# One row of an output-projection weight loaded by four smaller DMAs, and a shorter last sum, in a one-token decode kernel

## The chip, the core and the metric

The kernel runs on one core of one Trainium2 chip. A core has a matrix engine (PE in the profile, with its weight loads as PEld), a vector engine (DVE), a scalar engine (ACT), a general engine (POOL) and a sync engine (SP). SP and ACT issue the loads here; the bytes of all loads are moved by the core's 16 DMA engines. The metric is the device time of one execution in microseconds (us).

## What is computed

One token of width 1024 passes through two branches, which are added to the input. `xn` is the layer-normalised input.

```python
xn = _layernorm(x)
# attention over the last 4096 cached positions: 32 query heads, 4 key/value heads, head size 128
q = (xn @ wq)                                  # wq: 1024 x 4096
p = _softmax(q . k_cache[last 4096] * 128**-0.5)
o = p . v_cache[last 4096]                     # 32 heads x 128 = 4096 numbers
A = o @ wo                                     # wo: 4096 x 1024
# channel MLP
h = _gelu(_layernorm(xn) @ w1 + b1)            # w1: 1024 x 3584
B = h @ w2 + b2                                # w2: 3584 x 1024
out = x + A + B
```

The kernel computes in bfloat16 with float32 sums. With one token there is nothing to reuse: every weight and every cached key and value is read once, 39.9 MB in all.

## The kernel before, in words

**Loads.** All large loads are issued by SP in program order: the keys (four loads), wq (two), w1 (two), the values (three), w2 (two), wo (six). Each puts its matrix on 128 partitions. They go into a ring of four buffers of 32 KB per partition (`ring_tile`, line 64), so that a load waits until the work on the buffer's earlier content is done. The framework gives each DMA one of eight completion semaphores in rotation; a DMA waits until the DMA that used its semaphore before has landed. ACT issues three loads of single rows at the start: x, b2 and b1 (lines 75 to 78).

**wo.** wo has 4096 rows of 1024. Row `32 p + c` lies on partition `p` as its row `c` (`wo_v`, line 222), so each partition holds 32 rows of 2 KB, and a product with one column `c` of a 128 x 32 matrix `o8` takes one such row of all partitions at once. The first half (rows 0 to 15, buffer `wo0`) comes by one DMA, the second half (`wo1`) by five, of 8, 4, 2, 1 and 1 rows (lines 223 to 229), so that the last products wait for little.

**Attention.** The keys are transposed by DVE and copied by DVE and ACT (lines 184 to 201). Query, scores, softmax and the product with the values `o_all` (line 319) follow. DVE scales and gathers the result into `o_bf`, 32 heads x 128 (lines 322 to 326). Element `128 h + d` of the concatenated heads belongs to partition `p = 4 h + d // 32` and column `c = d % 32` of `o8`; four small products with a 0/1 matrix `spread` make `o8` of `o_bf` (lines 327 to 331). `spread` is made by POOL early on (lines 108 to 111), among POOL's other constants and before its two short steps `rstd` of the layer norms (lines 145 and 168).

**The last sum.** The 28 rows of w2 and the 32 rows of wo form a list `chunk_src` of 60 entries. All but the last `TAIL = 8` are summed into `accf`: two halves of 512 columns, each half in its own 32-row group of the matrix engine (lines 336 to 339), one row of output in partition 0 and one in partition 32. Then four copies, by DVE and ACT in turn, bring `accf` to `bulk`, in four pieces of 256 columns on partitions 0, 32, 64 and 96 (lines 344 to 350). The last eight rows, those that the second to fifth DMA of `wo1` bring, are summed into `acct` in four groups of 256 columns (lines 351 to 354). One addition of `acct` and `bulk` on DVE gives `res` (line 356), which SP stores as four rows of 512 bytes (line 357).

The matrix engine takes its instructions in the order of the program: w2's rows, then wo's rows 0 to 31. A group of products that waits for a load holds up all that follow.

Of the kernel before, what the change touches and what calls it, by code (L numbers as in the profile page):

```python
# [8 lines left out]
FP32 = mybir.dt.float32  # L9
BF16 = mybir.dt.bfloat16  # L10
ACT = mybir.ActivationFunctionType
ALU = mybir.AluOpType
# [4 lines left out]
def kernel(  # L17
# [14 lines left out]
    nc = tc.nc  # L32
    P = 128
    D = A_x.shape[-1]
# [4 lines left out]
    Hq = NQ // Dh  # L39
# [8 lines left out]
    CWO = NQ // P  # L48
    TAIL = 8
    NH = Fd // 8  # L50
# [4 lines left out]
    consts = ctx.enter_context(tc.tile_pool(name="consts", bufs=1))  # L55
# [4 lines left out]
    ps_f = ctx.enter_context(tc.tile_pool(name="ps_f", bufs=2, space=bass.MemoryType.PSUM))  # L60
# [23 lines left out]
    for i in range(2):  # L84
        t = ring_tile(f"wq{i}")
        tv = t[:].rearrange("p (r n) -> p r n", r=4)
# [23 lines left out]
    nc.gpsimd.affine_select(out=spread[:], in_=spread[:], compare_op=ALU.not_equal, fill=1.0, base=0,  # L110
                            pattern=[[-1, 4], [1, P]], channel_multiplier=-4)

    gmask = consts.tile([Hq, Hkv], FP32)
# [108 lines left out]
    wo_v = A_wo.rearrange("(p c) n -> p c n", p=P)  # L222
    for i, cuts in enumerate([[0, 16], [0, 8, 12, 14, 15, 16]]):
        nr = CWO // 2
        t = ring_tile(f"wo{i}")
        tv = t[:].rearrange("p (r n) -> p r n", r=nr)
        for a, b in zip(cuts[:-1], cuts[1:]):
            nc.sync.dma_start(out=tv[:, a:b, :], in_=wo_v[:, nr * i + a:nr * i + b, :])  # L228
        chunk_src += [("o", nr * i + r, tv[:, r, :]) for r in range(nr)]


    for i, w3 in enumerate(wq_tiles):
        for r in range(4):
            c = 4 * i + r
# [91 lines left out]
    nc.vector.tensor_copy(out=o_bf[:], in_=o_f[:])  # L326
    o8_ps = ps_f.tile([P, 32], FP32, tag="pf", name="o8_ps")
    for q in range(4):
        nc.tensor.matmul(o8_ps[:], lhsT=spread[:, q, :], rhs=o_bf[:, 32 * q:32 * q + 32], start=(q == 0), stop=(q == 3))
    o8 = consts.tile([P, 32], BF16)  # L330
    nc.vector.tensor_copy(out=o8[:], in_=o8_ps[:])

# [3 lines left out]
    for idx, (kind, c, wap) in enumerate(chunk_src[:n_bulk]):  # L336
        for half in range(2):
            nc.tensor.matmul(accf[32 * half:32 * half + 1, :], lhsT=vec[kind](c), rhs=wap[:, half * 512:(half + 1) * 512],  # L338
                             start=False, stop=(idx == n_bulk - 1), tile_position=(0, 32 * half))
    acct = ps_f.tile([P, 256], FP32, tag="pf", name="acct")  # L340
# [47 lines left out]
```

## Time and profile before

| | |
|---|---|
| median of three runs | 102.23 us (102.08 to 102.32) |
| the profiled execution's own time | 102.15 us |
| its span, from the first to the last instruction | 100.4 us |
| mean granted clock of the matrix engine | 0.846 |
| bytes moved, mean rate over the span | 39.92 MB, 397 GB/s |
| matrix engine busy | 45.7 us (45%) |
| DVE busy | 49.2 us (49%) |
| ACT busy | 34.2 us (34%) |
| POOL busy | 4.0 us (4%) |
| first of wo's second-half DMAs issued | 70.34 us |
| last addition (line 356) | 97.43 to 97.86 us |

All times of a profile are us from the first instruction; "L338" is line 338 of the kernel. A row of the timeline gives start, duration, engine, line, operation, output and inputs, shape and count, and in brackets how long the engine had been idle and what ended that. A row of the windows gives a stretch and its length, the busy time of PE, PEld, DVE, ACT and POOL with the number of instructions, the granted clock of the matrix engine, the mean busy share of the 16 DMA engines, and GB/s. Beside these views the trace holds every packet of a DMA (start, duration, size, queue) and every step of a completion semaphore. It does not say on which of the 16 DMA engines a packet ran.

### The profile page before, as it was taken

To read this page: it belongs to the slowest core of one execution; us is meant where nothing else is said; L and a number is where in the kernel's file an instruction comes from. 1 tells how busy PE (TensorE), PEld (TensorE's weight loads), DVE (VectorE), ACT (ScalarE), POOL (GpSimd) and SP (SyncE) were. 2 spreads that over 40 slices of the span, in tenths; PEclk is the share of its full clock that TensorE was granted. 3 is DMA by queue.
4 is the path that set the end of the run, shared out by engine and by line. 5 is a ranking of instruction groups with operands and counts; after the bars stand their busy time and mean duration, and the time that the engine had idled before them with its cause. 6 is when DMAs were issued, how large, how long until landed. Compare 5 with 4: busy or idle time off the path is not lost.

```text
span 100.4 us, 976 instructions
## 1 busy us (share of the span) xinstructions
PE 45.7 (45%) x369; PEld 18.0 (18%) x369; DVE 49.2 (49%) x91; ACT 34.2 (34%) x37; POOL 4.0 (4%) x17
## 2 busy tenths in 40 slices
PE   0472000009500920297462009999199910299640
PEld 0422000003100300024221003334133400033210
DVE  4616799999999999992552460000900000000310
ACT  2300008999999999902204630000000000000100
POOL 6024200000000000000000000000000000000000
PEclk9999999999999997559999655589957995559975
DMA  2999999999999998999999998989989999999900
GB/s 40 375 431 434 499 431 496 431 418 418 418 418 392 468 440 369 502 400 400 390 440 424 424 506 388 509 377 423 480 388 414 418 444 437 437 405 401 382 33 1
DMA packets 2882, 39.92 MB, mean 397 GB/s; under 512 B 311, under 2 KB 315, under 8 KB 702
## 3 DMA queue, kind: packets, MB, share of 16 engines
q1 hardware_dynamic: 2872, 39.85, 93.3%
q8 instruction: 3, 0.05, 0.2%
q10 hardware_dynamic: 6, 0.01, 0.0%
q14 instruction: 1, 0.01, 0.0%
HBM read 39.86 MB, written 0.00 MB: 397 GB/s over the span
## 4 chain that ended last, share of the span: by engine, by line
DVE 39%; DMA 25%; PE 15%; issue 8%; ACT 5%; POOL 3%; SPq 2%; POOLq 1%; ACTq 0%; DVEq 0%
DMA wo<-in_A_wo_dram 25%; DVE kt_scr L185 17%; DVE kT L201 16%; PE o_all L319 10%; PE sp L275 2%; DVE hT L314 2%; SPq L228 2%; PE acch L257 2%; ACT L312 1%; ACT e L297 1%; DVE eTb L299 1%; DVE m_loc L283 1%; ACT h_sb L312 1%; DVE q_sb L240 1%; POOLq L383 1%
## 5 line engine op out<-in xcount | busy, mean ns | idle before, releaser
L199 ACT COPY kT<-kt_scr 32x1024 bf16<-32x1024 bf16 x26 | 27.1, 1042 | 12.2 <-DVE kt_scr L185 12.0
L185 DVE STREAM_TRANSPOSE kt_scr<-k_sb 128x4096 bf16<-128x4096 bf16 x4 | 17.4, 4409 | 0.0
L201 DVE COPY kT<-kt_scr 32x1024 bf16<-32x1024 bf16 x38 | 15.9, 419 | 0.5
L237 PE MATMUL accq<-wq,xnT 128*1 128x512 bf16 x64 | 6.9, 607 | 19.5 <-DMA wq<-in_A_wq_dram 19.5
L350 ACT COPY bulk<-accf 1x256 f32<-1x256 f32 x2 | 0.7, 361 | 36.3 <-DVE bulk L348 36.3
L319 PE MATMUL o_all<-v_sb,eTb 128*32 128x512 bf16 x32 | 9.9, 484 | 5.4 <-DVE hT L314 5.4
L348 DVE COPY bulk<-accf 1x256 f32<-1x256 f32 x2 | 0.8, 416 | 21.6 <-PE accf L338 21.1
L338 PE MATMUL accf<-wo,o 128*1 128x512 bf16 x48 | 6.8, 449 | 6.5 <-DMA wo<-in_A_wo_dram 6.5
L338 PE MATMUL accf<-w,hT 128*1 128x512 bf16 x56 | 8.1, 452 | 0.1
L257 PE MATMUL acch<-w,yT 128*1 128x448 bf16 x64 | 4.8, 463 | 6.3 <-DMA w<-in_B_w_dram 6.3
L237 PEld LDWEIGHTS <-xnT 128*1 128x1 bf16 x64 | 2.1, 116 | 23.8 <-issue 23.8
L319 PEld LDWEIGHTS <-eTb 128*32 128x32 bf16 x32 | 3.7, 117 | 11.2 <-DVE hT L314 5.5
L322 DVE TENSOR_TENSOR o_m<-o_all,grs 32x512 f32<-32x512 f32 x1 | 0.7, 679 | 10.0 <-PE o_all L319 10.0
L338 PEld LDWEIGHTS <-o 128*1 128x1 bf16 x48 | 2.4, 94 | 10.9 <-issue 8.8
L338 PEld LDWEIGHTS <-hT 128*1 128x1 bf16 x56 | 2.8, 96 | 4.9 <-issue 2.7
L257 PEld LDWEIGHTS <-yT 128*1 128x1 bf16 x64 | 1.7, 99 | 9.0 <-issue 8.3
L314 DVE STREAM_TRANSPOSE hT<-h_sb 128x896 bf16<-128x896 bf16 x1 | 1.7, 1699 | 2.4 <-ACT h_sb L312 2.4
L297 ACT ACTIVATE e<-sc,nmx 128x1024 bf16<-128x1024 f32 x1 | 1.1, 1147 | 3.9 <-DVE nmx L294 3.9
L353 PE MATMUL acct<-wo,o 128*1 128x256 bf16 x32 | 1.7, 283 | 1.7 <-DMA wo<-in_A_wo_dram 1.7
L275 PE MATMUL sp<-kT,qm 128*32 128x512 bf16 x32 | 2.1, 380 | 0.3 <-DVE qm L266 0.3
L104 ACT ACT_TABLE_LOAD x1 | 1.3, 1283 | 1.9 <-issue 1.9
L299 DVE STREAM_TRANSPOSE eTb<-e 128x1024 bf16<-128x1024 bf16 x1 | 1.2, 1246 | 1.4 <-ACT e L297 1.4
(85 smaller groups left out, 32.2 us busy)
## 6 DMA issues: line engine op xcount, KB each, us to landing
w<-in_B_w_dram SPq DMA_DIRECT2D x4, 3584.0 KB, 23.7
wq<-in_A_wq_dram SPq DMA_DIRECT2D x2, 4096.0 KB, 19.9
k_sb<-in_A_k_cache_dram SPq DMA_DIRECT2D x4, 1024.0 KB, 7.0
wo<-in_A_wo_dram SPq DMA_DIRECT2D x1, 4096.0 KB
v_sb<-in_A_v_cache_dram SPq DMA_DIRECT2D x1, 2048.0 KB
v_sb<-in_A_v_cache_dram SPq DMA_DIRECT2D x2, 1024.0 KB, 22.5
wo<-in_A_wo_dram SPq DMA_DIRECT2D x1, 2048.0 KB, 21.6
wo<-in_A_wo_dram SPq DMA_DIRECT2D x1, 1024.0 KB
```

The lines of the kernel that those rows point to most:

```text
L185: nc.vector.transpose(out=scr[:, g, :], in_=k2[:, g, :])
L199: nc.scalar.copy(out=dst, in_=src)
L201: nc.vector.tensor_copy(out=dst, in_=src)
L228: nc.sync.dma_start(out=tv[:, a:b, :], in_=wo_v[:, nr * i + a:nr * i + b, :])
L237: nc.tensor.matmul(accq[32 * t:32 * t + 1, b, :], lhsT=xnT[:, c:c + 1], rhs=w3[:, r, j * 512:(j + 1) * 512], start=(c == 0), stop=(c == C ...
L257: nc.tensor.matmul(acch[32 * t:32 * t + 1, b, :NH], lhsT=yT[:, c:c + 1], rhs=w3[:, r, j * NH:(j + 1) * NH], start=False, stop=(c == C - 1) ...
L275: nc.tensor.matmul(sp[32 * R:32 * R + 32, :], lhsT=qm[:, g, :], rhs=kT[:, g, c0:c0 + 512], start=(g == 0), stop=(g == Hkv - 1), tile_posit ...
L297: nc.scalar.activation(out=e128[:], in_=sc[:], func=ACT.Exp, bias=nmx[:], scale=scale, accum_out=l_loc[:])
L299: nc.vector.transpose(out=eTb[:], in_=e128[:])
L314: nc.vector.transpose(out=hT[:], in_=h_sb[:].rearrange("p (d c) -> p c d", c=CW2))
L319: nc.tensor.matmul(o_all[:].rearrange("h g d -> h (g d)"), lhsT=eTb[:, 32 * c:32 * c + 32], rhs=v4[:, :, c, :], start=(c == 0), stop=(c == ...
L338: nc.tensor.matmul(accf[32 * half:32 * half + 1, :], lhsT=vec[kind](c), rhs=wap[:, half * 512:(half + 1) * 512], start=False, stop=(idx == ...
```

## The change

Row 15 of `wo0` is no longer part of the large DMA, which now brings rows 0 to 14. Four DMAs of their own follow it. Two bring row 15 of partitions 0 to 95 to where it was, the first on partitions 0, 2, 4 and so on, the second on 1, 3, 5. Two bring row 15 of the other 32 partitions (96 to 127) to partitions 0 to 31 of a new buffer `wo_x`, again every second partition each. Their source is cut so that its outermost count is 12 (for the 96) or 4 (for the 32): source rows are taken in groups of four partitions, every second group by one DMA. Partition `8 e + 2 v + s` therefore holds the row of partition `8 e + 4 s + v`. A second 0/1 matrix `spread_x` with four more small products makes a 33rd column of `o8` in that order, and a copy moves its partitions 96 to 127 to partitions 0 to 31 as a 34th. The two products of row 15 become four: two over 96 partitions and two over 32. `TAIL` goes from 8 to 4: rows 24 to 27, which the 4-row DMA brings, are summed into `accf`, and four rows are left for `acct`.

```diff
--- before.py
+++ after.py
@@ -46,7 +46,7 @@
     WQ4 = W // 4
     CW2 = Fd // P
     CWO = NQ // P
-    TAIL = 8
+    TAIL = 4
     NH = Fd // 8
     eps = 1e-5
     scale = float(Dh) ** -0.5
@@ -109,6 +109,12 @@
     nc.gpsimd.memset(spread[:], 0.0)
     nc.gpsimd.affine_select(out=spread[:], in_=spread[:], compare_op=ALU.not_equal, fill=1.0, base=0,
                             pattern=[[-1, 4], [1, P]], channel_multiplier=-4)
+    spread_x = consts.tile([Hq, 4, P], BF16)
+    nc.gpsimd.memset(spread_x[:], 0.0)
+    for s in range(2):
+        sx = spread_x[:].rearrange("h q (e a s) -> h q e a s", a=4, s=2)[:, :, :, :, s]
+        nc.gpsimd.affine_select(out=sx, in_=sx, compare_op=ALU.not_equal, fill=1.0, base=4 * s,
+                                pattern=[[-1, 4], [8, 16], [1, 4]], channel_multiplier=-4)
 
     gmask = consts.tile([Hq, Hkv], FP32)
     nc.gpsimd.memset(gmask[:], 1.0)
@@ -220,12 +226,20 @@
         nc.sync.dma_start(out=tv, in_=w2_v[:, nr * i:nr * (i + 1), :])
         chunk_src += [("h", nr * i + r, tv[:, r, :]) for r in range(nr)]
     wo_v = A_wo.rearrange("(p c) n -> p c n", p=P)
-    for i, cuts in enumerate([[0, 16], [0, 8, 12, 14, 15, 16]]):
+    MOVED = 15
+    wo_x = consts.tile([32, D], BF16)
+    for i, cuts in enumerate([[0, MOVED], [0, 8, 12, 14, 15, 16]]):
         nr = CWO // 2
         t = ring_tile(f"wo{i}")
         tv = t[:].rearrange("p (r n) -> p r n", r=nr)
         for a, b in zip(cuts[:-1], cuts[1:]):
             nc.sync.dma_start(out=tv[:, a:b, :], in_=wo_v[:, nr * i + a:nr * i + b, :])
+        if i == 0:
+            wo_m = tv[:, MOVED, :]
+            for (dst, p0, ne) in ((wo_m, 0, 12), (wo_x, 96, 4)):
+                rows = A_wo[p0 * CWO:(p0 + 8 * ne) * CWO, :].rearrange("(e s v c) n -> e s v c n", e=ne, s=2, c=CWO)
+                for s in range(2):
+                    nc.sync.dma_start(out=dst[s:8 * ne:2, :], in_=rows[:, s, :, MOVED, :])
         chunk_src += [("o", nr * i + r, tv[:, r, :]) for r in range(nr)]
 
 
@@ -324,19 +338,27 @@
     nc.vector.tensor_reduce(out=o_f[:], in_=o_m[:].rearrange("h g d -> h d g"), axis=AX.X, op=ALU.add)
     o_bf = consts.tile([Hq, Dh], BF16)
     nc.vector.tensor_copy(out=o_bf[:], in_=o_f[:])
-    o8_ps = ps_f.tile([P, 32], FP32, tag="pf", name="o8_ps")
+    o8_ps = ps_f.tile([P, 33], FP32, tag="pf", name="o8_ps")
     for q in range(4):
-        nc.tensor.matmul(o8_ps[:], lhsT=spread[:, q, :], rhs=o_bf[:, 32 * q:32 * q + 32], start=(q == 0), stop=(q == 3))
-    o8 = consts.tile([P, 32], BF16)
-    nc.vector.tensor_copy(out=o8[:], in_=o8_ps[:])
+        nc.tensor.matmul(o8_ps[:, 0:32], lhsT=spread[:, q, :], rhs=o_bf[:, 32 * q:32 * q + 32], start=(q == 0), stop=(q == 3))
+    for q in range(4):
+        nc.tensor.matmul(o8_ps[:, 32:33], lhsT=spread_x[:, q, :], rhs=o_bf[:, 32 * q + MOVED:32 * q + MOVED + 1],
+                         start=(q == 0), stop=(q == 3))
+    o8 = consts.tile([P, 34], BF16)
+    nc.vector.tensor_copy(out=o8[:, 0:33], in_=o8_ps[:])
+    nc.vector.tensor_copy(out=o8[0:32, 33:34], in_=o8_ps[96:128, 32:33])
 
 
     vec = {"h": lambda c: hT[:, c, 0:1], "o": lambda c: o8[:, c:c + 1]}
     n_bulk = len(chunk_src) - TAIL
     for idx, (kind, c, wap) in enumerate(chunk_src[:n_bulk]):
-        for half in range(2):
-            nc.tensor.matmul(accf[32 * half:32 * half + 1, :], lhsT=vec[kind](c), rhs=wap[:, half * 512:(half + 1) * 512],
-                             start=False, stop=(idx == n_bulk - 1), tile_position=(0, 32 * half))
+        parts = [(vec[kind](c), wap)]
+        if kind == "o" and c == MOVED:
+            parts = [(o8[0:96, 32:33], wo_m[0:96, :]), (o8[0:32, 33:34], wo_x)]
+        for (lh, rh) in parts:
+            for half in range(2):
+                nc.tensor.matmul(accf[32 * half:32 * half + 1, :], lhsT=lh, rhs=rh[:, half * 512:(half + 1) * 512],
+                                 start=False, stop=(idx == n_bulk - 1), tile_position=(0, 32 * half))
     acct = ps_f.tile([P, 256], FP32, tag="pf", name="acct")
     nc.vector.memset(acct[:], 0.0)
     bulk = consts.tile([97, 256], FP32)
```

In the built program POOL's memset and two selects for `spread_x` stand before its first `rstd`. The semaphore rotation moves on by four. The DMAs of `wo1` then wait, in order, for the third load of the values (as well as for the buffer), for w2's first half, for w2's second half, for the first half of wo, and for the first of the four new DMAs.

## The prediction

> **What bounds the kernel now.** I read the page first. The line of transfers is at nine tenths or more almost from start to end, and the matrix engine works 45% of the span: the kernel moves 39.9 MB and ends soon after the last byte of wo is in. So I went to the last 25 us: the timeline of the matrix engine there, the windows over the same stretch, and the waits.
>
> ```profile
> 87.15 6.76 PE L338 MATMUL accf<-wo,o 128*1 128x512 bf16 x48 [6.47 <-DMA wo<-in_A_wo_dram]
> 94.45 0.61 PE L353 MATMUL acct<-wo,o 128*1 128x256 bf16 x16 [0.54 <-DMA wo<-in_A_wo_dram]
> 95.68 0.39 PE L353 MATMUL acct<-wo,o 128*1 128x256 bf16 x8 [0.62 <-DMA wo<-in_A_wo_dram]
> 96.29 0.28 PE L353 MATMUL acct<-wo,o 128*1 128x256 bf16 x4 [0.22 <-DMA wo<-in_A_wo_dram]
> 96.93 0.38 PE L353 MATMUL acct<-wo,o 128*1 128x256 bf16 x4 [0.36 <-DMA wo<-in_A_wo_dram]
> ```
>
> Each group of the last sum starts when its wo rows land; the last at 96.93. What follows (products to 97.31, the addition 97.43 to 97.86, the store, the end at 100.4) has nothing beside it. A later or earlier last landing moves the end by the same amount.
>
> ```profile
> 92.00:94.00 2.00, 1.91 (x18) 0.62 (x15) 0.05 (x1) 0.00 (x0) 0.00 (x0) 1.00 0.97 400
> 94.00:95.50 1.50, 0.61 (x16) 0.37 (x17) 0.79 (x2) 0.56 (x2) 0.00 (x0) 1.00 0.89 344
> 95.50:97.00 1.50, 0.74 (x16) 0.34 (x15) 0.00 (x0) 0.16 (x1) 0.00 (x0) 0.96 0.14 51
> ```
>
> The last two columns are the busy share of the 16 DMA engines and GB/s. Until 95.5 they are all at work; then 0.14, two or three of 16, hold the end for over a microsecond. A load over 128 partitions raises its semaphore in 16 steps, one per engine. For the last wo row the trace's records put 12 steps at 95.38 to 95.69, then 95.81, **96.25, 96.72 and 96.89**. Following the packets of one engine back (each starts where the one before ended), the three late ones lost their time to instruction packets: 16 KB at 37.07 and at 63.95, on two engines, each losing 1.42 us in all (0.92 of its own and 0.5 on the next packet), and 8 KB at 38.18 on a third (0.84). A fourth engine takes 16 KB at 95.51, when its data are in. The 95.81 engine is the one that also carried the single-row loads of x and the biases; I call it engine 0.
>
> **The change, part by part.** *The moved row.* A row of wo is 2 KB on each of 128 partitions, eight packets per engine, 0.080 us apart at the end of the trace: 0.64 us. How many engines do the four new DMAs use? The store of four rows is four 512-byte packets, x's single row one packet: the outer count sets it. The new DMAs' sources have outer counts 12, 12, 4 and 4 (their destinations 48 and 16). So I take 12 engines, eight packets over two DMAs, and then four of these with eight more. The other end is all 16 engines with eight each: then nothing moves.
>
> Terms per engine. Before, wo's first half came in 32 KB packets every 1.209 us; 28 KB packets come every 1.059, so 30 KB is 1.134 by the middle: 8 x 0.075 = 0.60 less for every engine. Added for the twelve: 8 x 0.080 and two semaphore packets of 0.006 = 0.65. Added again for the four: 0.65. **Relieved (four engines): -0.60. Middle (eight): +0.05. Loaded (four): +0.70.** Engine 0 is among the loaded, as the single rows ride on it: 95.81 + 0.70 = 96.51.
>
> [...]
>
> *Whether the late engines are the relieved ones decides all*, and no view numbers them. For it: fetches fall on four different engines, never on engine 0, as if four were set apart, and four away from engine 0 are relieved. Against: the first packets of k_sb start at 1.86 to 2.10 us on 12 engines and at 2.86 to 2.90 on four; the late engines are among the 12, and if start order were engine order the relieved would be the other four. I choose "relieved", with little over even odds against everything else: this is the weakest step.
>
> With it the last landings become 96.89 - 0.60 = 96.29, 96.12, and engine 0 at 96.51. Last: 96.51, **0.38 earlier**. The two ends of this term: -0.60 (engine 0 not loaded) and +0.70.
>
> *Four rows instead of eight in the last sum.* Rows 24 to 27 go into accf: 8 products of 512 columns replace 16 of 256. They run in pairs 0.2135 us apart at full clock, the last taking 0.38: 3 x 0.2135 + 0.38 = 1.02. Their rows landed at 94.41 on the last engine; after: engine 0, 93.24 + 0.70 = 93.94. So accf ends at 93.94 + 0.05 + 1.02 = 95.01. The four copies to bulk (DVE and ACT in turn) took 93.95 to 95.66 = 1.71; they end at 96.76. The last products end at 96.51 + 0.04 + 0.38 = 96.93. So the copies stay covered by 0.17; their cover was 1.65. If they are the later, each 0.1 us costs 0.1. PE itself: 29 pairs of wo instead of 24, from 86.55; at half clock (0.427 a pair) until 90.05, then 0.2135: it would end near 94.6, before its rows let it.
>
> *What is covered.* Pool gains a memset (0.51) and two selects of half of L110's size (0.3 to 0.63 each) ahead of the first rstd: at most 1.8 into 4.63 us of waiting.
>
> ```profile
> 7.01 0.56 POOL L145 TENSOR_TENSOR rstd<-ve,mhalf 128x1 f32<-128x1 f32 x1 [4.63 <-DVE ve L143]
> 72.37 0.25 PE L329 MATMUL o_ps<-o_bf,spread 32*128 32x32 bf16 x4 [2.06 <-DVE o_bf L326]
> ```
>
> Four more products like L329's (0.25) and one more copy of o8 (0.19) lie ahead of PE's wait of 6.47 for wo and of 21.1 us of idle DVE. SP issues four more DMAs at 0.43 each after 52.92, and idles until 70.34; its queue is deep, since wo's first packets move only at 75.5. The rotation of eight DMA semaphores shifts, so wo's second-half parts now wait: the third for w2 (landed 77.45), the fourth for the first half of wo (86.5 to 87.1), the fifth for the first moved DMA (about 87). Behind them in SP's queue stands only the store. Their first packets are wanted at 92.5, 93.8 and 94.4: over five us of cover; were it gone, a late issue would cost what it is late by.
>
> Unknown: what 2 KB packets cost that land on every second partition beside other engines' packets. From nothing to as much again on the loaded four: 0 to +0.64; no row suggests a gain. I take 0, as the 2 KB rows at the end ran 0.080 apart with 16 engines writing.
>
> **Sum:** -0.38. The profiled execution was 102.15 us (span 100.4, 1.75 around it), the median of the runs shown 102.23. 102.15 - 0.38 = 101.77, so **101.8**; its own range 101.5 to 101.95 (ends -0.60 and -0.2, when a third of the unknown cost falls on engine 0).
>
> **Rivals.** (1) *The time was in none of the relieved engines*, or only one of the two latest is relieved, or all 16 share the moved row: last landing 96.89 + 0.05 at most: 102.15 to 102.25, no change. The same comes out if the packets on the loaded engines cost over half more.
> (2) *A late engine is one of the loaded four.* Its 0.70 comes on top of the latest: 96.89 + 0.70 = 97.59, or 96.72 + 0.70 = 97.42; with the tail unchanged +0.53 to +0.70: 102.7 to 102.85. It decides as soon as an engine later than 96.19 (96.89 - 0.70) is loaded; the early start of the late engines speaks for it.
> (3) *The copies to bulk become the end*: by the sum 0.17 short; if rows 24 to 27 land after 94.1, it takes a part of the gain, and in (1) it adds nothing (97.28 against 97.36).
>
> **How the numbers follow.** Chances: forecast 0.50; (1) 0.18; (2) 0.32. (3) is inside the forecast. A measurement of this kernel can tell about 0.2% (0.2 us) from no change: faster 0.48 (the forecast less its slow end), same 0.20, slower 0.32. The range 101.5 to 102.85 takes in all three; the likeliest alone is 101.5 to 101.95.
>
> **What would show it.** Right: the last L353 group starts near 96.55 and the share of the DMA engines after 95.5 shows more engines for a shorter time; the 16 steps of the last wo row have one near 96.5 and none past it; the first moved DMA shows 12 steps. Wrong: three steps still past 96.2, in the same distance (1), or one past 97.4 (2); an addition that waits for ACT's copy and not for PE (3); or a matrix engine that waits for a wo part issued late.

## The result, and the profile after

The changed kernel takes 103.29 us (median of 4 runs, 103.09 to 103.43); the kernel before, beside it, 102.28 us (4 runs, 102.08 to 102.34). The ratio is 1.0105 with a 95% interval of 1.0084 to 1.0127: about 1.0 us slower, where 0.4 us faster was forecast, and outside the range given. The profiled execution took 103.09 us with a span of 101.4 us (before: 102.15 and 100.4).

The timeline of the matrix engine over the last 12 us, in the changed kernel:

```profile
87.33 5.99 PE L360 MATMUL accf<-wo,o 128*1 128x512 bf16 x32 [4.89 <-DMA wo<-in_A_wo_dram]
93.25 0.38 PE L360 MATMUL accf<-wo_x,o 32*1 32x512 bf16 x2
93.56 2.87 PE L360 MATMUL accf<-wo,o 128*1 128x512 bf16 x24
96.62 0.39 PE L375 MATMUL acct<-wo,o 128*1 128x256 bf16 x8 [0.20 <-DMA wo<-in_A_wo_dram]
97.23 0.28 PE L375 MATMUL acct<-wo,o 128*1 128x256 bf16 x4 [0.22 <-DMA wo<-in_A_wo_dram]
97.85 0.28 PE L375 MATMUL acct<-wo,o 128*1 128x256 bf16 x4 [0.34 <-DMA wo<-in_A_wo_dram]
```

The picture is that of before: each group of the last sum starts when its rows land, and the last starts at 97.85 instead of 96.93. In the records of semaphore steps the last row of wo is complete at 97.81 instead of 96.89. So the 0.92 us are there before the last product starts; its products end 0.82 later than before (98.13 for 97.31), and the addition starts 0.82 later.

The windows over the same kernel; behind the stretch and its length stand PE, PEld, DVE, ACT and POOL, and at the end the granted clock, the busy share of the DMA engines, and GB/s:

```profile
85.00:86.50 1.50, 0.00 (x0) 0.00 (x0) 0.00 (x0) 0.00 (x0) 0.00 (x0) 0.61 1.25 388
86.50:88.00 1.50, 0.67 (x4) 0.21 (x5) 0.00 (x0) 0.00 (x0) 0.00 (x0) 0.50 0.84 277
...
94.00:95.50 1.50, 1.50 (x16) 0.59 (x14) 0.00 (x0) 0.00 (x0) 0.00 (x0) 1.00 1.06 421
95.50:97.00 1.50, 1.30 (x16) 0.36 (x13) 0.41 (x1) 0.03 (x1) 0.00 (x0) 1.00 0.52 201
97.00:98.50 1.50, 0.57 (x12) 0.17 (x7) 0.67 (x2) 0.69 (x2) 0.00 (x0) 1.00 0.02 7
```

The same two first stretches in the kernel before:

```profile
85.00:86.50 1.50, 0.00 (x0) 0.00 (x0) 0.00 (x0) 0.00 (x0) 0.00 (x0) 0.50 0.84 360
86.50:88.00 1.50, 0.85 (x6) 0.26 (x7) 0.00 (x0) 0.00 (x0) 0.00 (x0) 0.50 1.15 492
```

A packet counts whole in the stretch in which it starts, so a share can pass 1.00. What is to be read is GB/s divided by the share, the rate that 16 engines have while they are busy. Before it is 360 / 0.84 = 429 and 492 / 1.15 = 428. After it is 388 / 1.25 = **310** and 277 / 0.84 = **330**, and from 94.00 on 421 / 1.06 = 397, as before the change (344 / 0.89 = 387 in the row that the prediction shows). The DMA engines are not idle; for three microseconds each byte takes about a third longer. No term of the prediction stands for this. I call it the slow spell.

The packet records show it packet by packet: the moved row's 2 KB packets take 84 ns each if they start before 85.46, then up to 209 ns. The first 16 KB packet of wo's second half starts at 84.81 and takes its usual 611 ns; the next starts at 85.16 and takes 804, and from 85.4 on, on every engine that has come to them, they take 810 to 970. At 87.46 the last packet of `wo_x` has run, and those that start then fall from 760 back to 611 ns by 88.0. All that the packets between 84.7 and 88 took beyond their usual length is 12.2 us, or 12.2 / 16 = **0.76 us per engine**.

The vector engine, and ACT's second copy, at the end of the changed kernel:

```profile
96.47 0.41 DVE L370 COPY bulk<-accf 1x256 f32<-1x256 f32 x1 [23.94 <-PE accf L360]
97.36 0.42 DVE L370 COPY bulk<-accf 1x256 f32<-1x256 f32 x1 [0.48 <-ACT bulk L372]
98.25 0.42 DVE L378 TENSOR_TENSOR res<-acct,bulk 97x256 bf16<-97x256 f32 x1 [0.47 <-ACT bulk L372]
```

```profile
97.82 0.36 ACT L372 COPY bulk<-accf 1x256 f32<-1x256 f32 x1 [0.48 <-DVE bulk L370]
```

The last copy ends at 98.18, the last products at 98.13, and the view names the copy as what the addition waited for, the sign that the prediction gave for its third rival. Before, 0.12 us lay between the products' end and the addition; here 98.13 + 0.12 = 98.25 as well. So the copies have used up all their cover, but cost nothing that can be seen in this execution.

### The profile page after: what moved, and what is told of

It reads as the page before. It is cut to its first block, busy times and chain, and to the rows that moved or that the text cites. A ratio compares the mean times of both kernels' runs of the same rounds, so it can differ in the third digit from the quotient of the medians.

```text
span 101.4 us, 982 instructions
## 1 busy us (share of the span) xinstructions
PE 47.6 (47%) x367; PEld 18.8 (19%) x367; DVE 49.6 (49%) x92; ACT 34.2 (34%) x37; POOL 6.3 (6%) x20
## 4 chain that ended last, share of the span: by engine, by line
DMA 79%; PE 12%; SPq 2%; DVE 2%; issue 1%; ACT 1%; DVEq 0%
DMA wo<-in_A_wo_dram 44%; DMA wq<-in_A_wq_dram 20%; DMA w<-in_B_w_dram 15%; PE acch L271 5%; PE accq L251 4%; PE sp L289 3%; SPq L73 2%; DVE m_loc L297 1%; PE qT_ps L275 1%; ACT sc L294 1%; DVE res L378 0%; SPq L236 0%; DVE qm L280 0%; PE acct L375 0%; PE mT_ps L299 0%
## 5 line engine op out<-in xcount | busy, mean ns | idle before, releaser
L333 PE MATMUL o_all<-v_sb,eTb 128*32 128x512 bf16 x32 | 9.2, 458 | 5.2 <-DMA v_sb<-in_A_v_cache_dram 5.2
L360 PE MATMUL accf<-wo,o 128*1 128x512 bf16 (+1 forms) x56 | 8.9, 480 | 4.9 <-DMA wo<-in_A_wo_dram 4.9
L360 PEld LDWEIGHTS <-o 128*1 128x1 bf16 (+2 forms) x58 | 2.8, 99 | 11.2 <-issue 9.8
L289 PEld LDWEIGHTS <-qm 128*32 128x32 bf16 x32 | 1.7, 112 | 1.0 <-issue 0.6
```

What stands on the lines that cost most here:

```text
L289: nc.tensor.matmul(sp[32 * R:32 * R + 32, :], lhsT=qm[:, g, :], rhs=kT[:, g, c0:c0 + 512], start=(g == 0), stop=(g == Hkv - 1), tile_posit ...
L333: nc.tensor.matmul(o_all[:].rearrange("h g d -> h (g d)"), lhsT=eTb[:, 32 * c:32 * c + 32], rhs=v4[:, :, c, :], start=(c == 0), stop=(c == ...
L360: nc.tensor.matmul(accf[32 * half:32 * half + 1, :], lhsT=lh, rhs=rh[:, half * 512:(half + 1) * 512], start=False, stop=(idx == n_bulk - 1 ...
```

## The experiments

The result left these causes open: the shorter last sum (`TAIL = 4`); the moved row's own extra packets on a few engines; and something in the way the moved row is loaded that slows all engines for a while. Later runs divide the last one further: uneven counts of engines; every second partition; which rows a DMA engine reads, or which partitions it writes, beside the other engines. The table gives all runs; "rate" is GB/s by share from the windows row of 85 to 88 us in the profiled execution, "last" the last semaphore step of wo there. Ratios are to the kernel before, which had medians of 102.11 to 102.28 beside them. The diffs show the lines that load; the lines that fit the products and `spread_x` to them are left out.

| kernel | median us | ratio (95%) | rate | last |
|---|---|---|---|---|
| before | 102.28 | | 426 | 96.89 |
| after | 103.29 | 1.0105 (1.0084 to 1.0127) | 320 | 97.81 |
| e1_tail4_only | 102.37 | 1.0021 (0.9993 to 1.0048) | 428 | 97.12 |
| e2_rows_only | 103.96 | 1.0155 (1.0094 to 1.0215) | 301 | 99.01 |
| e3_home_dest | 103.66 | 1.0147 (1.0083 to 1.0210) | 322 | 97.64 |
| e4_swapped_groups | 103.43 | 1.0103 (1.0063 to 1.0142) | 297 | 98.30 |
| e5_no_four_engine | 103.57 | 1.0111 (1.0051 to 1.0171) | 304 | 98.01 |
| e6_plain_slices | 103.73 | 1.0145 (1.0128 to 1.0162) | 313 | 98.17 |
| e7_only_four_engine | 103.74 | one run | 324 | 98.55 |
| e8_plain_row15 | 102.21 | 0.9993 (0.9980 to 1.0007) | 423 | 96.72 |
| e9_two_halves | 103.33 | 1.0132 (1.0104 to 1.0159) | 308 | 98.11 |
| e10_source_mixed | 103.26 | one run | 297 | 98.15 |
| e11_last_row_uneven | 103.09 | 1.0107 (1.0092 to 1.0121) | 426 | 97.26 |
| f4_own_source_rows | 103.31 | 1.0108 (1.0061 to 1.0155) | 309 | 98.17 |
| f1_every_second | 102.28 | 1.0003 (0.9983 to 1.0023) | 421 | 97.07 |
| f2_dest_only | 103.40 | 1.0100 (1.0066 to 1.0135) | 304 | 98.25 |
| f5_extra_home | 102.44 | 1.0014 (1.0002 to 1.0026) | 419 | 97.44 |
| f7_extra_away | 103.07 | 1.0078 (1.0057 to 1.0099) | 339 | 97.63 |

"Last" belongs to one execution, in which instruction packets come at slightly other times (the 8 KB packet at 38.18 us in the kernel before, at 37.17 in the changed kernel), and that execution can lie at either end of a kernel's runs; the rates and the medians carry the verdicts.

### The two halves of the change alone

The kernel before, with the shorter last sum only:

```diff
-    TAIL = 8
+    TAIL = 4
```

> The kernel before with four rows instead of eight in the last sum, and no moved row. Theory (the loss comes from the moved row's DMAs): the four copies to bulk end at 94.46 + 1.02 + 0.05 + 1.71 = 97.24, the last products at 97.31 as before, so 102.2 to 102.4. Rival (the shorter last sum makes the copies the end, and that is the loss): 102.9 to 103.3.

102.37 us, a ratio whose interval takes in 1, and a rate of 428: no spell, and in the median at most half a per cent for the shorter last sum. But the profiled execution, at 103.08 us the slowest of the ten, is the rival's case:

```profile
97.16 0.28 PE L353 MATMUL acct<-wo,o 128*1 128x256 bf16 x4 [0.28 <-DMA wo<-in_A_wo_dram]
```

```profile
96.61 0.41 DVE L348 COPY bulk<-accf 1x256 f32<-1x256 f32 x1 [23.75 <-PE accf L338]
98.35 0.42 DVE L356 TENSOR_TENSOR res<-acct,bulk 97x256 bf16<-97x256 f32 x1 [0.43 <-ACT bulk L350]
```

The last products end at 97.44, so the addition could have started at 97.44 + 0.12 = 97.56; it waits for the copies until 98.35, which costs 0.79 us. Rows 24 to 27 had landed at 94.67; it was the matrix engine that was late. Its pairs of products of 512 columns stood 0.43 us apart until 93.4, and 0.21 us from then on; in the kernel before the change of pace came at 90.1, in the changed kernel at 92.0. From 90 to 92 us the granted clock was 0.50 here and 0.99 in the kernel before. Two more of the ten runs took 102.98 and 103.01 us, the other seven 101.97 to 102.55; whether those two had the same cause was not recorded. So the shorter last sum makes no spell, but it can cost 0.8 us in single executions.

The changed kernel with the last sum of eight rows:

```diff
-    TAIL = 4
+    TAIL = 8
```

> The changed kernel with eight rows in the last sum again, so that only the moved row is left of the change. Theory (moved row): a spell near 85.4 to 87.5 us in which the 16 KB packets of all engines take 0.83 to 0.97 us instead of 0.61, the last wo row landing near 97.8, 103.0 to 103.3. Rival (the shorter last sum): the last row still lands near 97 and the time is 102.2 to 102.4.

103.96 us: the moved row alone is enough for all the loss, as each of the four runs (103.31 to 104.47) is slower than any of the kernel before, and the spell is there (301). In this profile the packets stayed about a tenth slower after it, too: between 88 and 92 us the rate is 381 where after has 427.

### Where the moved row lands, and who is loaded

The 32 rows of `wo_x` go to partitions 96 to 127, where they were before, instead of 0 to 31; one product pair then takes row 15.

```diff
-            for (dst, p0, ne) in ((wo_m, 0, 12), (wo_x, 96, 4)):
+            for (dst, p0, ne) in ((tv[0:96, MOVED, :], 0, 12), (tv[96:128, MOVED, :], 96, 4)):
```

> As the changed kernel, but the rows of partitions 96 to 127 stay on partitions 96 to 127 (every second one, by the same two DMAs on four engines), with one product of 128 partitions for row 15. If the slow spell comes from writing on partitions 0 to 31 beside other engines' writes, it goes away: 16 KB packets 0.61 throughout, last landing 96.95 (the engine with the 8 KB instruction packet, 96.25 + 0.70), 102.2 to 102.4. If it comes from four engines reading rows that are not their own, or from any load on four engines beside full loads, the spell stays and the time is 103.0 to 103.3.

103.66 us, rate 322: the spell is untouched. Loading another partition than the row's own is not what makes it.

The two groups are exchanged: 12 engines load partitions 32 to 127, four load 0 to 31.

```diff
-            for (dst, p0, ne) in ((wo_m, 0, 12), (wo_x, 96, 4)):
+            for (dst, p0, ne) in ((tv[32:128, MOVED, :], 32, 12), (tv[0:32, MOVED, :], 0, 4)):
```

> As the changed kernel, but the two DMAs on 12 engines bring partitions 32 to 127 and the two on four engines partitions 0 to 31, all to their own partitions. If engines serve fixed groups of partitions and only rows away from their own group are slow, the four-engine part is now at home and fast (no spell after 85.4) and the 12-engine part is the one that could be slow (its 2 KB packets over 0.10 us). If any load on four engines slows all, the spell stays as it was and the time is 103.0 to 103.3; without any spell 102.2 to 102.4.

103.43 us, rate 297. The spell doesn't depend on which rows the 12 and the four take.

### Which of the four DMAs, and whether any

Only the 12-engine pair is kept; the other 32 rows come by one plain DMA (with `TAIL = 8`).

```diff
+            for s in range(2):
+                rows = A_wo[0:96 * CWO, :].rearrange("(e s v c) n -> e s v c n", e=12, s=2, c=CWO)
+                nc.sync.dma_start(out=tv[s:96:2, MOVED, :], in_=rows[:, s, :, MOVED, :])
+            nc.sync.dma_start(out=tv[96:128, MOVED, :], in_=wo_v[96:128, MOVED, :])
```

> Row 15 without the two DMAs on four engines: partitions 0 to 95 by the two DMAs on 12 engines as changed, partitions 96 to 127 by one DMA of 32 rows on all 16 engines, two packets each; eight rows in the last sum. Theory (four engines alone with 2 KB packets while the others have gone on to 16 KB packets slow all 16): no spell, 16 KB packets 0.61 throughout; relieved engines 0.60 - 0.16 = 0.44 earlier, the others 0.21 later, the last wo row near 96.5, 101.8 to 102.1. Rival (the spell comes from the 12-engine DMAs, or from 2 KB packets of any kind in front of 16 KB packets): the spell stays and the time is 103 to 104.

103.57 us, rate 304. Only the four-engine pair is kept, and the 96 rows come by one plain DMA (`TAIL = 8`):

```diff
+            nc.sync.dma_start(out=tv[0:96, MOVED, :], in_=wo_v[0:96, MOVED, :])
+            for s in range(2):
+                rows = A_wo[96 * CWO:128 * CWO, :].rearrange("(e s v c) n -> e s v c n", e=4, s=2, c=CWO)
+                nc.sync.dma_start(out=tv[96 + s:128:2, MOVED, :], in_=rows[:, s, :, MOVED, :])
```

> Row 15 of partitions 0 to 95 by one DMA on all 16 engines (six packets each), of partitions 96 to 127 by the two DMAs on four engines; eight rows in the last sum. Theory (four engines alone): the spell is there in full, 16 KB packets at 0.83 to 0.97 us for as long as the four engines have 2 KB packets, the last wo row at 97.5 or later, about 103.0 or more. Rival (12-engine DMAs): no spell, about 102.3.

103.74 us in one run, rate 324, and again a slower rest (382 between 88 and 92). Neither pair is needed for the spell, if the one run of the second kernel can be trusted. Both kernels have a plain DMA of fewer than 128 partitions in place of the pair that went; two such DMAs have the spell by themselves in e9 below (308).

Unless said otherwise, the kernels from here on are the kernel before with the first half of wo cut at row 15 and that row loaded in the way that the diff shows. First in consecutive slices, no partition skipped:

```diff
+            for p, pe in ((0, 72), (72, 96), (96, 120), (120, 128)):
+                nc.sync.dma_start(out=tv[p:pe, 15, :], in_=wo_v[p:pe, 15, :])
```

> The kernel before, with row 15 loaded to its own partitions by four DMAs of consecutive partitions (72, 24, 24 and 8), so that no engine writes every second partition; if the engine count is the largest up to 16 that divides the outer count, they run on 12, 12, 12 and 8 engines, relieving four engines of 0.60, and loading the others by 0.05 to 0.30. No additional product, eight rows in the last sum. Theory (four engines alone): no or little spell, the last wo row between 96.3 and 96.6, 101.7 to 102.0. Rival (a load on fewer than 16 engines slows all others): a spell, 102.8 or more. Rival (every second partition is what is slow): no spell.

103.73 us, rate 313. The semaphores show 12, 12, 12 and 8 steps. So skipping partitions is not needed for the spell either.

Row 15 as a DMA of its own over all 128 partitions:

```diff
-    for i, cuts in enumerate([[0, 16], [0, 8, 12, 14, 15, 16]]):
+    for i, cuts in enumerate([[0, 15, 16], [0, 8, 12, 14, 15, 16]]):
```

> The kernel before with row 15 as one DMA of its own over 128 partitions, eight 2 KB packets on every engine, nothing moved. Theory (uneven loads): no spell, all engines 0.05 later (eight packets of 0.080 for 8 x 0.075, one more semaphore packet), 102.2 to 102.4. Rival (2 KB packets in front of 16 KB packets are enough): a spell as in the changed kernel, 102.8 or more.

102.21 us, ratio 0.9993. The windows of this kernel:

```profile
85.00:86.50 1.50, 0.15 (x2) 0.09 (x3) 0.00 (x0) 0.00 (x0) 0.00 (x0) 0.63 1.07 444
86.50:88.00 1.50, 1.50 (x8) 0.40 (x6) 0.00 (x0) 0.00 (x0) 0.00 (x0) 0.50 1.10 470
```

444 / 1.07 = 415 and 470 / 1.10 = 427: 2 KB packets at this place, and one DMA more, do no harm in this load over all 128 partitions.

### Even counts, and the source alone

Row 15 as two DMAs of 64 partitions, on 16 engines each by the 16 steps that loads of 64 partitions raise in f2 below, so that every engine has eight packets as before:

```diff
+            for p in (0, 64):
+                nc.sync.dma_start(out=tv[p:p + 64, 15, :], in_=wo_v[p:p + 64, 15, :])
```

> [...] Theory (an engine that reads or writes rows of another engine's usual partitions slows the others while these load theirs): a spell from the first 16 KB packets (85.5) until the latest engine has its 2 KB packets (87), 16 KB packets over 0.8 us, 102.6 to 103.5. Rival (loads on fewer engines, or uneven ones, are the cause): no spell, 102.2 to 102.4.

```profile
85.00:86.50 1.50, 0.00 (x0) 0.00 (x0) 0.00 (x0) 0.00 (x0) 0.00 (x0) 1.00 1.21 350
86.50:88.00 1.50, 0.36 (x2) 0.09 (x3) 0.00 (x0) 0.00 (x0) 0.00 (x0) 0.87 0.91 304
```

350 / 1.21 = 289, 304 / 0.91 = 334, and 103.33 us. This run shows that uneven counts are not needed: by that count no engine has more packets than before, and the loss is 1.3%. What differs from e8 is that each DMA loads one half of the partitions, and that there are two DMAs (as there are in f1 below, without a spell). Which engine has which partition the trace doesn't tell.

Row 15 by one DMA over all 128 partitions, but with its source in another order (partition 8 e + v gets the row of partition 16 v + e, so row 15's products use the wrong elements of `o8`):

```diff
+            mixed = A_wo.rearrange("(v e c) n -> e v c n", e=16, c=CWO)
+            nc.sync.dma_start(out=tv[:, 15, :], in_=mixed[:, :, 15, :])
```

> The kernel before with row 15 as one DMA over 128 partitions whose source rows are taken in another order (partition 8 e + v gets the row of partition 16 v + e), so that only the reading side differs from the usual; row 15 of the product is mixed by this. If reading rows away from the usual is what slows: a spell of 16 KB packets over 0.8 us near 85.5 to 87, 102.6 or more. If the writing side or uneven counts are the cause: no spell, 102.1 to 102.4.

```profile
85.00:86.50 1.50, 0.00 (x0) 0.00 (x0) 0.00 (x0) 0.00 (x0) 0.00 (x0) 0.86 1.23 354
86.50:88.00 1.50, 0.42 (x4) 0.12 (x5) 0.00 (x0) 0.00 (x0) 0.00 (x0) 0.50 0.84 265
```

354 / 1.23 = 288, 265 / 0.84 = 315, and 103.26 us in one run. The destination is that of e8, partition by partition. So another order of the source is enough for the spell, though one DMA covers all 128 partitions. That only the reading side has changed is not shown, however: the source now has an outer count of 16 instead of 128, and the trace doesn't tell which engine writes which partition.

### At the end instead of the middle

The last row of all (row 31) in the slices of e6, where no further load follows; the first half of wo is whole again:

```diff
+            for p, pe in ((0, 72), (72, 96), (96, 120), (120, 128)):
+                nc.sync.dma_start(out=tv[p:pe, 15, :], in_=wo_v[p:pe, nr + 15, :])
```

> The kernel before with the very last wo row (31) loaded by four DMAs of 72, 24, 24 and 8 partitions, on 12, 12, 12 and 8 engines, so that the four relieved engines skip 0.64 us and no full load follows the uneven one. Theory (the slow spell needs full loads beside the uneven ones): the spell is limited to the time in which the late relieved engines still load row 30 and before; the last step of row 31 near 96.3 to 96.6 instead of 96.9, 101.7 to 102.0. Rival (uneven loads cost more than the relief gives, wherever they stand): 102.4 or more.

```profile
95.00:96.50 1.50, 0.08 (x4) 0.00 (x0) 0.52 (x2) 0.72 (x2) 0.00 (x0) 1.00 0.51 130
```

130 / 0.51 = 255 GB/s, where before has 117 / 0.32 = 366 in this stretch. The spell comes here too: 60 packets that start between 95 and 96 us take 2.9 us more in all, or 0.18 us per engine, and the last row lands at 97.26 instead of 96.89. The median is 103.09 us, ratio 1.0107. The profiled execution was the fastest of the six (102.46 us), so what the slower ones lost beyond this is not seen. This is no way to relieve the late engines either.

### Which rows an engine reads, which partitions it writes

Here I supposed that an engine serves eight consecutive partitions in a load of 128, which no trace shows. The changed kernel, its four-engine DMAs reading the rows of partitions 0 to 31 once more (row 15 of partitions 96 to 127 is left out of the sum, and that of 0 to 31 taken in its place):

```diff
-                rows = A_wo[p0 * CWO:(p0 + 8 * ne) * CWO, :].rearrange("(e s v c) n -> e s v c n", e=ne, s=2, c=CWO)
+                rows = A_wo[0:8 * ne * CWO, :].rearrange("(e s v c) n -> e s v c n", e=ne, s=2, c=CWO)
```

> The changed kernel, but the two DMAs on four engines read row 15 of partitions 0 to 31 a second time (still into the new buffer on partitions 0 to 31), not that of 96 to 127; the term of row 15 for the last 32 partitions is therefore another. Counts per engine, destinations, products: all as in the changed kernel. Theory (an engine reading rows that other engines usually read slows all): no spell, 16 KB packets 0.61; the per-engine sum of the prediction then holds: relieved -0.60, the four +0.70, and as the engine with the 8 KB instruction packet is one of the four, the last step is near 96.95, 102.1 to 102.4. Rival (uneven loads slow all): the spell stays, 103.0 or more.

103.31 us, rate 309. Under the supposition every engine of the four DMAs now reads and writes at its own eight partitions, and still the spell stayed. So either the supposition is wrong, or whose rows they are doesn't matter; no run decides between these. The last pair of runs asks only whether the place matters when the counts are the same.

Row 15 by two DMAs of every second partition, 16 engines each, source and destination alike:

```diff
+            for s in range(2):
+                nc.sync.dma_start(out=tv[s:128:2, 15, :], in_=wo_v[s:128:2, 15, :])
```

> The kernel before with row 15 by two DMAs over every second partition (0, 2, 4 ... and 1, 3, 5 ...), on all 16 engines, so that an engine has the same eight partitions as in the large loads if these go by eight consecutive partitions per engine. Theory (rows read away from the usual engine): no spell, 102.2 to 102.4, where the two halves of consecutive partitions had one. If engines are not tied to eight consecutive partitions: a spell and 103 or more.

```profile
85.00:86.50 1.50, 0.00 (x0) 0.00 (x0) 0.00 (x0) 0.00 (x0) 0.00 (x0) 0.55 1.16 483
86.50:88.00 1.50, 1.25 (x8) 0.37 (x9) 0.00 (x0) 0.00 (x0) 0.00 (x0) 0.50 1.00 426
```

483 / 1.16 = 416, 426 / 1.00, and 102.28 us, ratio 1.0003: no spell. Every second partition is harmless here. The same source with the rows laid on partitions 0 to 63 and 64 to 127 (row 15's products then pair rows with other elements of `o8`):

```diff
+            for s in range(2):
+                nc.sync.dma_start(out=tv[64 * s:64 * s + 64, 15, :], in_=wo_v[s:128:2, 15, :])
```

> As the run with every second partition on the reading side, but written to partitions 0 to 63 and 64 to 127 in order, so that only the writing side is away from the usual; row 15 of the product is mixed by this. Theory (the reading side alone): no spell, 102.2 to 102.4. If the writing side does it as well: a spell, 102.8 or more.

```profile
85.00:86.50 1.50, 0.00 (x0) 0.00 (x0) 0.00 (x0) 0.00 (x0) 0.00 (x0) 1.00 1.16 328
86.50:88.00 1.50, 0.21 (x2) 0.09 (x3) 0.00 (x0) 0.00 (x0) 0.00 (x0) 0.83 0.96 317
```

328 / 1.16 = 283, 317 / 0.96 = 330, and 103.40 us. The reads and all counts are those of f1, and both of its loads raise 16 steps, so all 16 engines write to each half of the partitions. If the counts settle which engine takes which row, only the writing side has changed, and that is enough for the spell.

The last pair of runs keeps the counts and changes the place. Both are e8 with two small DMAs more, of 16 rows each, into a buffer that nothing uses; they differ in two numbers. In f5 the loop is over partitions 0 and 32, as here; in f7 it is over 16 and 48. The sources of the small DMAs have an outer count of 4, as those of the last two moved DMAs of the changed kernel, which raise 4 steps, so I take four engines for each. That they are the same four in both runs is assumed, and so is what the theories below take as own partitions and as those of other engines: the trace names no engine, and no run shows which partitions an engine serves.

```diff
+            for p in (0, 32):
+                rows = A_wo[p * CWO:(p + 16) * CWO, :].rearrange("(e r) n -> e r n", r=4 * CWO)
+                nc.sync.dma_start(out=extra[p:p + 16, :], in_=rows[:, 12:112:33, :])
```

> Row 15 as one plain load of 128 partitions (which was free of a spell), and after it two more loads of 16 rows each on four engines into a scratch buffer that nothing reads: partitions 0 to 15 and 32 to 47. So the four engines have eight 2 KB packets more, as in the change. [...] Theory (own partitions cost nothing beyond their packets): no spell, the four engines 0.65 later, the last step 96.9 to 97.0, 102.2 to 102.5. Rival (uneven counts alone slow all 16): a spell, 103 or more.

> [...] Theory (partitions of other engines): a spell of 16 KB packets over 0.8 us from 85.5 to about 87, the last step 0.5 to 1.0 later than in the run before, 102.9 to 103.6. Rival (counts alone decide): the same time as the run before.

The windows of f5, then of f7:

```profile
85.00:86.00 1.00, 0.00 (x0) 0.00 (x0) 0.00 (x0) 0.00 (x0) 0.00 (x0) 0.58 1.28 522
86.00:87.00 1.00, 0.00 (x0) 0.00 (x0) 0.00 (x0) 0.00 (x0) 0.00 (x0) 0.50 0.87 367
87.00:88.00 1.00, 0.92 (x6) 0.33 (x7) 0.00 (x0) 0.00 (x0) 0.00 (x0) 0.50 1.01 432
```

```profile
85.00:86.00 1.00, 0.00 (x0) 0.00 (x0) 0.00 (x0) 0.00 (x0) 0.00 (x0) 1.00 1.25 442
86.00:87.00 1.00, 0.00 (x0) 0.00 (x0) 0.00 (x0) 0.00 (x0) 0.00 (x0) 0.98 1.04 279
87.00:88.00 1.00, 0.85 (x6) 0.26 (x7) 0.00 (x0) 0.00 (x0) 0.00 (x0) 0.50 0.93 367
```

In the middle second line f5 has 367 / 0.87 = 422 GB/s, f7 279 / 1.04 = **268**. In f5 every 16 KB packet takes 611 ns; in f7 they take up to 1065, and its packets lose 9.9 us in all, 9.9 / 16 = 0.62 us per engine. The medians are 102.44 (1.0014, interval 1.0002 to 1.0026) and 103.07 (1.0078, interval 1.0057 to 1.0099): 0.63 us between them. The two profiled executions, of 102.63 and 102.81 us, are closer, and their last rows land only 0.19 us apart: in f5's another engine, without extra packets, came to its row 15 only at 86.61 and ended last. So the 0.63 us rests on the medians. Counts of DMAs, rows and bytes, and the shapes of the loads, are the same. It is the choice of partitions that makes the spell, and as f1 and e8 load partitions 16 to 31 and 48 to 63 without one, these are not slow by themselves. The extra packets alone cost 0.14%.

## Why the prediction was wrong

**What is shown.** Placement decides, and not counts: f5 and f7 differ in nothing but the partitions (422 and 268 GB/s by share between 86 and 87 us), and e9, with even counts, has the spell (289 and 334). Three ways of loading row 15 in the middle kept the rate: one plain load (e8, 423), two loads of every second partition (f1, 421), and the plain load with the small ones of f5 behind it (419). All others lost it, at 297 to 339. In the changed kernel the 16 KB packets that started between 85.4 and 87.3 took 0.81 to 0.97 us instead of 0.61, and the length fell back once the last 2 KB packet was through at 87.46. That the writing side is enough follows from f2, with the condition named there; whether the reading side alone would be is open, since e10 may have changed both. The theory that several of the runs were made for, that each engine has rows of its own in the loads of 128 partitions and that engines at the rows of others slow all, is not shown: the trace names no engine, and no run tells which engine serves which partition.

**The step that failed** is the one on the unknown: "what 2 KB packets cost that land on every second partition beside other engines' packets. From nothing to as much again on the loaded four: 0 to +0.64 ... I take 0". The runs put 0.76 us per engine in its place, and 0.86 on the engine that was last. The bound was wrong in kind, not only in size: it let the packets hurt the engines that carry them and no other, while the cost falls on all 16, on the relieved ones too. The row chosen for "0", 2 KB packets 0.080 apart "with 16 engines writing", was of a load over 128 partitions, which in e8 has no spell either (415 and 427); it could not show this. And the reason feared, every second partition, is free (f1, ratio 1.0003).

**A smaller step had failed as well.** "Engine 0 is among the loaded ... 95.81 + 0.70 = 96.51", the last landing, left out that the engine of the 8 KB fetch, last at 96.25, might be loaded as well. That engine 0 is loaded stayed an estimate; the engine of the 8 KB fetch is: in the packet records it carries the moved packets of all four DMAs and ends last. 96.25 + 0.70 = 96.95 is 0.06 later than before, so that even at full rate the change would by the prediction's own terms have brought nothing. In its packet chain the 16 KB packets end at 92.48, at 90.92 before: 1.56 later, which is the 0.70 of the sum and 0.86 of spell, and 96.25 + 1.56 = 97.81 is the last step measured. Rival 2 named the condition for it (an engine later than 96.19 among the loaded) but priced only the two latest.

**Right, point by point.**
- The last landing moves the end: 97.81 - 96.89 = 0.92, and the profiled execution is 103.09 - 102.15 = 0.94 longer. Of this 0.82 stands at the addition's start and still at the store's last step (99.54 and 100.36); what is left comes after the store has landed and was not followed up.
- The moved DMAs show 12, 12, 4 and 4 steps, and the slices of e6 12, 12, 12 and 8.
- The weakest step held for the two latest engines: they are among the relieved. The prediction gave this little over even odds, so it was luck as much as reasoning. In the packet chains they go from 30 KB packets straight to 16 KB packets. They gained the 0.60 and lost more to the spell: their 16 KB packets end at 91.70 and 91.92, before the change at 91.44 and 91.61.
- The middle engines' 16 KB part took 5.58 us instead of 4.86 for eight packets that follow each other without a gap: +0.05 was forecast, 0.72 of spell comes on top.
- The four copies took 96.47 to 98.18 = 1.71 us, as forecast, and rows 24 to 27 landed at 95.36 instead of 93.94, hence the used-up cover. It cost nothing in this execution. But the sum took it that the matrix engine leaves half clock at 90.05, as in the one profile of before, and would end near 94.6; it left it at 92.0 here and at 93.4 in e1, where the copies then cost 0.79 us. The 0.17 of cover was too small for that, and the third rival can be the end.
- The later wo DMAs were issued at 77.54 and 87.30, when the DMAs before them on their semaphores had landed, and at 87.68, right behind; no engine ran dry for it.

**Mis-sized but covered.** POOL's constants took more than "at most 1.8 into 4.63 us of waiting". The timeline of POOL in the changed kernel:

```profile
2.31 0.51 POOL L113 MEMSET spread_x<- 32x512 bf16 x1
2.79 0.62 POOL L110 TENSOR_SCALAR_AFFINE_SELECT spread<-spread 32x512 bf16<-32x512 bf16 x1
3.38 1.74 POOL L116 TENSOR_SCALAR_AFFINE_SELECT spread_x<-spread_x 32x256 bf16<-32x256 bf16 x2
6.93 0.56 POOL L151 TENSOR_TENSOR rstd<-ve,mhalf 128x1 f32<-128x1 f32 x1 [1.73 <-DVE ve L149]
```

The two selects took 1.74 us together, 0.87 each instead of 0.3 to 0.63, and the memset 0.51. The select of `spread` (0.62), which stood behind `rstd` in the kernel before, now stands ahead of it too. `rstd` still waits 1.73 us, where it waited 4.63, so all of this was hidden.

**What stays open.** Why all 16 engines slow down, and not only those that carry the moved row, is not known, nor what about a place or an order makes the spell, nor whether another order of reading alone is enough. Nor is why in e2, e6 and e7 the packets stayed a tenth slower after the spell (16 KB packets mostly at 681 to 684 instead of 611 ns; rates of 381 to 383 between 88 and 92 us against 422 to 429 in the others). No version here beat the kernel before: e1, e8 and f1 are level with it. To relieve a late engine another engine must take some of its bytes, and every version that did so had the spell, in the middle (e2, rate 301) as at the end (e11, 255 where before has 366).

## What to carry to other kernels

In a kernel that is bound by its loads, load a part of a matrix in the shape of the loads beside it, and measure any other shape by itself: one row in slices (e6, ratio 1.0145), in two halves of 64 partitions (e9, 1.0132) or from a source in another order (e10, 103.26 us) slowed the transfers here and cost about 1% of the whole, though it moved a sixtieth of wo's and w2's rows; as one plain load it cost nothing (e8, 0.9993). Read GB/s divided by the engines' busy share, stretch by stretch; a fall there (429 to 310) means that the transfers themselves have become slower, which neither the busy share nor the count of bytes shows. And when a cost is unknown, ask first on whom it can fall: a bound that names too few engines is too small whatever its number.

## What the runs showed of the hardware

- Row 15 in four DMAs of 12, 12, 4 and 4 steps, beside the next full load, lengthened 16 KB packets from 0.611 to 0.81 to 0.97 us between 85.4 and 87.3 us (changed kernel); another place of writing was enough (f2, 283 GB/s per share where f1 has 416), and so was another order of the source (e10, 288 where e8 has 415). In the changed kernel a 16 KB packet that one engine started at 84.81, while most others were at 2 KB packets, still took 0.611 us, and the 2 KB packets before 85.46 took their usual 84 ns.
- The same number of 2 KB packets, in two DMAs of 16 rows, cost 0.14% on partitions 0 to 15 and 32 to 47 (f5) and 0.78% on 16 to 31 and 48 to 63 (f7).
- The instruction fetches in the kernel before ride on engines that carry the data: 16 KB cost its engine 1.42 us and 8 KB 0.84 us, and the three engines that took one between 37 and 64 us end last. In the changed kernel those of the two 16 KB fetches were among the four that a DMA of 12 leaves out, that of the 8 KB fetch among the four that a DMA of four uses.
- The moment at which the matrix engine goes from half to full clock in the last sum differs between executions: pairs of 512-column products went from 0.43 to 0.21 us apart at 90.1 us in the kernel before, at 92.0 in the changed kernel and at 93.4 in e1.
